# Linear attention and a SwiGLU feed-forward on one core: one block's k and v sent for ahead of a down phase, q moved by one transfer a product, basis blocks written later, the VectorE in program order

## The chip, the core and the metric

The kernel runs on one core of a Trainium2 chip. The core has five engines with a queue of instructions each: the TensorE (PE in the profile; its weight loads are PEld), the VectorE (DVE), the ScalarE (ACT), GpSimd (POOL) and SyncE (SP), which here only issues transfers. Transfers run on 16 DMA engines. SBUF is the core's working memory, PSUM holds the results of matmuls. An engine that needs another's result waits on a semaphore. The metric is the device time in microseconds of one execution.

## The reference

Eight batches, eight heads, a sequence of 576, 64 elements a head, all in FP32. Attention is linear: no softmax.

```python
kv  = np.einsum('bhsd,bhse->bhde', k, v)           # 64 x 64 per batch and head
out = np.einsum('bhsd,bhde->bhse', q, kv)
rms = np.sqrt(np.mean(out * out, axis=-1, keepdims=True) + 1e-06)
x   = (out / rms * g_norm).transpose(0, 2, 1, 3).reshape(4608, 512)
g   = x @ w_gate                                    # 512 x 1536
h   = g / (1 + exp(-g)) * (x @ w_val)               # w_val 512 x 1536
y   = h @ w_out                                     # w_out 1536 x 512
```

Nearly all the arithmetic is in the three products with the weights.

## The kernel before

**Blocks.** The 4608 tokens are nine blocks of 512. For each block the attention part makes x, then the feed-forward has an *up* phase (both products with x, SiLU and the product of the two, giving h) and a *down* phase (h times w_out). Blocks 0, 1 and 2 run alone, the rest in pairs (3, 4), (5, 6), (7, 8). The attention work for the next blocks is slipped between the feed-forward's products of the current one.

**Fewer multiplications.** Block 0's up phase is plain. Block 1's uses one level of the Strassen-Winograd scheme: seven products of sums of blocks in place of eight (L629). Block 2 and the pairs use two levels. That needs *basis blocks*, sums of sub-blocks of the weights. They are made once, during block 1, and written to a tile `w` in HBM (L970), 512 KB a transfer; two groups of them (`owed_sends`) stay in an SBUF region called `arena` at first and are written only later. Block 2 and the pairs read basis blocks back from `w` through a ring of tiles `t` (L930, L933, L941), nine deep: a read waits until the product that used the slot nine reads before is done.

**Block 2's up phase.** Twelve units; each runs seven products (L797). A result leaves PSUM by an addition on the VectorE (L132) or by a copy on the ScalarE (L811) and additions from SBUF; GpSimd does the multiplications and some additions that make h (L134, L132). The loop at L1131 does three things after each product: it makes the next pieces of sums ready (`make`), takes one *chore* from a list (a VectorE or ScalarE step of the attention for the coming block), and takes *sends* from another list. A send is one quarter transfer of q (L315), 32 of them a block, alternately on SyncE's and the ScalarE's queue. Before the change it takes two sends a product.

Units are counted from 0 here. After a unit a function from a table is called; the table's key is the number of units done, so key 6 stands between unit 5 and unit 6. `ahead` (L1278 to L1322) builds this table from the attention of block 3 (`att`) and of block 4 (`then`):

- `visits` (key 1): matmuls k^T v of block 3 (a *visit*, L352); first half of block 3's q put into the sends.
- `second` (key 2): second half of block 3's q; first half of block 4's k and v asked for (`load_kv`, L294).
- `turn` (key 5): first visit to block 4's k, v; second half of block 4's k and v asked for; block 3's two q transposes (`turn_q`, L368) put into the chores.
- keys 6 and 8: the heads' products q kv (`half`, L407) for each half of block 3, with their chores (squares L421, root L437 to L452), and the two halves of block 4's q put into the sends.
- keys 9 and 10: x transposed (`turn_x`, L467), for each half.
- `last` (key 11): second visit to block 4's k, v; the two owed groups of basis blocks written, four transfers.

A visit can only use k and v once they are in; k, v and q of a block share SBUF slots with earlier ones, so a `load_kv` also waits for the last reader of what was there.

**Down phase.** Seven products of the outer level, each of parts (L629), with a table of functions called after a product. x of the next block is multiplied with the gain (L497), placed into the layout that the two-level scheme wants by 16 transfers (`place_x`, L490), and summed. `inner_sums` makes sums of sums of block 3's x for the pair; it is called after product 5 of block 2's down phase.

**What sets the order.** The program is traced in the order in which Python runs it, and a planner then arranges each engine's instructions by its own estimate of when they can start; it may move an instruction ahead of others on its engine where no data forbids it. `tc.issue_after(i)` forbids what it encloses to stand ahead of instruction i. Transfers issued on one queue go out in that queue's order.

Of the kernel before, what the change touches and what calls it, by code (L numbers as in the profile page):

```python
# [1 line left out]

# [16 lines left out]
def kernel(  # L19
# [41 lines left out]
    nc = tc.nc  # L61
# [47 lines left out]
    def span(at, size):  # L109

        return arena[:, int(at * KIB) : int((at + size) * KIB)]
# [17 lines left out]
    PAIRED = 3  # L129
# [2 lines left out]
    add = lambda e, o, a, b: e.tensor_tensor(out=o, in0=a, in1=b, op=OP.add)  # L132
    sub = lambda e, o, a, b: e.tensor_tensor(out=o, in0=a, in1=b, op=OP.subtract)  # L133
    mul = lambda e, o, a, b: e.tensor_tensor(out=o, in0=a, in1=b, op=OP.mult)  # L134

    def ring():

        return r_pool.tile([P, 4, BLK], F32, name="r")
# [75 lines left out]
    class Att:  # L214
# [246 lines left out]
        def turn_x(self, i):  # L461
            xt = self.xts[:, i].rearrange("p t j u d -> p t j (u d)")
            for j in range(0, NS, 2):
                ps = m_psum.tile([P, 2, 2, P], F32, name="m")
                for e in range(2):
                    for t in range(2):
                        self.turned_x = nc.tensor.transpose(ps[:, e, t], xt[:, t, j + e], ident)  # L467
                self.copied = nc.scalar.activation(
                    out=self.x[:, 2 * i + j // 2], in_=ps.rearrange("p e t c -> p e (t c)"), func=ACT.Copy, scale=gain
                )  # L470
# [51 lines left out]
        def half(self, i, pools=None):  # L522
            self.product(i, pools)
            self.root(i)
            self.scale(i)
            self.halves.append(self.scaled)
# [434 lines left out]
    owed_sends = []  # L961
# [118 lines left out]
    class Ffn:  # L1080
# [27 lines left out]
        def up(self, fill):  # L1108

            self.s1 = s_pool.tile([P, NP, HB], F32, name="s1")  # L1110
            units = []
            for d in range(NP // 2):
                if self.n < DEEP:
                    units += [Up(self, 2 * d), Up(self, 2 * d + 1)]
                else:
                    shared = {}
                    units += [Inner(self, d, g, shared) for g in range(4)]
            units[0].prepare()
            last = None
            for i, this in enumerate(units):  # L1120
                if i + 1 < len(units):
                    units[i + 1].prepare()
                for unit, p in this.sequence(last):
                    if unit:
                        visited, self.visited = self.visited, None
                        with tc.issue_after(visited.ins) if visited else ExitStack():
                            unit.multiply(p)
                        self.make(4)
                        if self.chores:
                            self.chores.pop(0)()  # L1130
                        for _ in range(2):  # L1131
                            if self.sends:
                                self.sends.pop(0)()
                last = this
                fill.get(12 * (i + 1) // len(units), lambda: None)()
            self.down_ = Down(self)
            self.down_.turn_t(5)
            for unit, p in last.sequence(None):
                if unit is None:
                    last.multiply(p)  # L1140
# [109 lines left out]
    def weights(upto):  # L1250
        nonlocal rounded
        while rounded < min(upto, len(pieces)):
            load_weights(rounded + 4)
            round_w(*pieces[rounded])
            rounded += 1

    def t2(place, b22, b11):

        sub(nc.vector, place, b22, place)
        add(nc.vector, place, place, b11)  # L1260

    blocks = [Att(n) for n in range(NB)]
# [7 lines left out]
    def visit(ffn, att, gs, apart=False):  # L1270

        with tc.issue_after(ffn.multiplied.ins):
            for g in gs:
                att.kv(g, apart)
        if att.n < B:
            ffn.visited = att.positions

    def ahead(ffn, att, then):  # L1278

        def load(att, i, *pairs):  # L1280
            ffn.sends += att.quarter_steps(i, pairs, (nc.sync, nc.scalar))

        def visits():
            visit(ffn, att, (0, 1))
            load(att, 0, 0, 1)

        def second():
            load(att, 1, 0, 1)
            then.load_kv(0)

        def turn():
            visit(ffn, then, (0,), True)
            then.load_kv(1)
            ffn.chores += [lambda i=i: att.turn_q(i) for i in range(2)]

        def half(i):
            with tc.issue_after(ffn.multiplied.ins):
                att.heads(i, range(NS), (m_psum, m_psum))
            ffn.visited = att.multiplied
            ffn.chores += att.chores(i)  # L1300

        def turn_x(i):
            with tc.issue_after(ffn.multiplied.ins):
                att.turn_x(i)
            ffn.visited = att.turned_x
            if i == 1:
                ffn.chores += att.sum_steps()

        def last():
            visit(ffn, then, (1,), True)  # L1310
            while owed_sends:
                owed_sends.pop(0)()

        att.homes = {
            "qt": h_alone[:, 8:12], "sq": span(0, 8).rearrange("p (f t) -> p f t", f=4),
            "xts": span(8, 8).rearrange("p (f t) -> p f t", f=4),
        }

        return {
            1: visits, 2: second, 5: turn, 6: lambda: (half(0), load(then, 0, 0, 1)),  # L1320
            8: lambda: (half(1), load(then, 1, 0, 1)), 9: lambda: turn_x(0), 10: lambda: turn_x(1), 11: last,
        }  # L1322

    for n in range(PAIRED):
        ffn = Ffn(n, blocks[n])
        nxt = blocks[n + 1]
        if n == 0:

            with tc.issue_after(squared.ins), tc.issue_after(scaled.ins):
                weights(2)  # L1330
            ffn.plain_up(0, (0,))
            copied = blocks[0].copied
            blocks[0].turn_x(1)
            for f in range(NF):
                with tc.issue_after(blocks[0].copied.ins if f else copied.ins):
                    weights(2 * (f + 2))
                ffn.plain_up(f) if f else ffn.plain_up(0, (1,))
            weights(len(pieces))
            pairs = wo.rearrange("p (j e) d -> p e j d", e=2)
            t2(pairs[:, 0, :, HD:DM], pairs[:, 1, :, HD:DM], pairs[:, 0, :, 0:HD])  # L1340
            nxt.room = xi_alone.rearrange("p a b c -> p (a b c)")

            with tc.issue_after(sent.ins):
                for i in range(2):
                    nxt.load_kv(i)
                for i in range(2):
                    nxt.load_q(i)
            ffn.plain_end()
            for g in range(2):
                nxt.kv(g)  # L1350
            nxt.turn()
        elif n == 1:

            def third():
                visit(ffn, nxt, (0,))
                nxt.load_kv(1)

            def two_thirds():
                visit(ffn, nxt, (1,))
                for i in range(2):  # L1360
                    nxt.load_q(i)

            ffn.up({4: third, 8: two_thirds})
            nxt.turn()
            blocks[PAIRED].load_kv(0)
        else:
            ffn.up(ahead(ffn, nxt, blocks[PAIRED + 1]))
            nxt = blocks[PAIRED + 1]
            nxt.turn()
            for g in range(2):  # L1370
                blocks[PAIRED + 2].load_kv(g)
        if n:
            ffn.down_.opens = n + 1

        def inner_sums():
            with tc.issue_after(ffn.multiplied.ins):
                blocks[PAIRED].inner_sums()

        ffn.down(nxt, {5: inner_sums} if n == 2 else {})
        if n == 1:  # L1380
            blocks[PAIRED].load_kv(1)
        if n == 0:
            blocks[2].load_kv(0)

            with tc.issue_after(nxt.halves[0].ins):
                for j in range(NP // 2):
                    t2(wv[j][:, 0:2], wv[j][:, 2:4], wg[j][:, 0:2])
            with tc.issue_after(ffn.down_.s4.ins):
                for j in range(NP // 2, NP):
                    t2(wv[j][:, 0:2], wv[j][:, 2:4], wg[j][:, 0:2])  # L1390
# [60 lines left out]
```

## Time and profile before

| | us |
|---|---|
| median of 3 runs | 1029.87 |
| lowest, highest | 1029.16, 1031.26 |
| the profiled execution, own time | 1032.78 |
| its span in the profile | 1031.0 |
| TensorE busy (97% of the span) | 1000.9 |
| VectorE busy (66%) | 685.1 |
| GpSimd busy (35%) | 362.5 |
| ScalarE busy (22%) | 229.0 |
| mean granted TensorE clock, share of full speed | 0.993 |

The profile records one execution. The chain of waits follows the work that ended last back to its start and gives each engine its share. The busy times by stretch have, for each row: the stretch in us from the span's start and its length, then busy time and instructions of TensorE, its weight loads, VectorE, ScalarE and GpSimd, then the granted clock, the share of time in which the DMA engines were busy, and GB/s. A row of the timeline has the start, the duration, the engine (SPq is SyncE's queue), the line, the operation, what it writes and reads, its shape and number and, in brackets, how long the engine stood before it and what ended that. A row of waits has the instruction's engine, result and line, what it waited for, the total wait, how many there were, and the longest.

### The profile page before, as it was taken

To read this page: it belongs to the slowest core of one execution; us is meant where nothing else is said; L and a number is where in the kernel's file an instruction comes from. 1 tells how busy PE (TensorE), PEld (TensorE's weight loads), DVE (VectorE), ACT (ScalarE), POOL (GpSimd) and SP (SyncE) were. 2 spreads that over 40 slices of the span, in tenths; PEclk is the share of its full clock that TensorE was granted. 3 is DMA by queue.
4 is the path that set the end of the run, shared out by engine and by line. 5 is a ranking of instruction groups with operands and counts; after the bars stand their busy time and mean duration, and the time that the engine had idled before them with its cause. 6 is when DMAs were issued, how large, how long until landed. Compare 5 with 4: busy or idle time off the path is not lost.

```text
span 1031.0 us, 17747 instructions
## 1 busy us (share of the span) xinstructions
PE 1000.9 (97%) x6774; PEld 844.1 (82%) x6774; DVE 685.1 (66%) x1166; ACT 229.0 (22%) x357; POOL 362.5 (35%) x283
## 2 busy tenths in 40 slices
PE   5999999999978999999999999999999999999998
PEld 4544688888978988888888888888888888888887
DVE  2998788988547795666667656666776566666211
ACT  2665111221202311111211211211212112121100
POOL 0000363434024531355565102465652025556600
PEclk9999999999989999999999999999999999999999
DMA  8689543667989746586742464667403545543011
GB/s 216 203 258 262 118 91 136 223 210 207 254 178 223 220 122 162 147 231 158 179 133 62 110 135 144 163 169 181 126 10 75 120 150 162 154 143 105 1 41 41
DMA packets 255637, 155.20 MB, mean 151 GB/s; under 512 B 141632, under 2 KB 234816, under 8 KB 255552
## 3 DMA queue, kind: packets, MB, share of 16 engines
q1 hardware_dynamic: 215104, 148.95, 52.9%
q10 hardware_dynamic: 40384, 5.12, 3.2%
q8 instruction: 54, 0.88, 0.4%
q14 instruction: 31, 0.25, 0.1%
q0 software_dynamic: 64, 0.00, 0.0%
HBM read 117.97 MB, written 28.70 MB: 142 GB/s over the span
## 4 chain that ended last, share of the span: by engine, by line
PE 72%; DMA 3%; DVE 1%; SPq 0%; issue 0%; ACT 0%; ACTq 0%; DVEq 0%
PE b L797 24%; PE b L629 16%; PE c L797 12%; PE c L629 8%; PE a L797 6%; PE a L629 4%; DMA t<-w 1%; PE m L407 1%; PE m L352 1%; DMA ld<-in_v_dram 1%; DMA ld<-in_q_dram 1%; DMA w<-arena 0%; DVE r L132 0%; SPq L970 0%; PE m L467 0%
## 5 line engine op out<-in xcount | busy, mean ns | idle before, releaser
L797 PE MATMUL b<-arena,t 128*128 128x256 f32 (+1 forms) x1248 | 280.9, 364 | 11.6 <-DMA t<-w 9.2
L797 PEld LDWEIGHTS b<-arena,t 128*128 128x128 f32 x1248 | 221.9, 192 | 42.8 <-DMA t<-w 7.0
L132 POOL TENSOR_TENSOR r<-r 128x256 f32<-128x256 f32 (+1 forms) x105 | 111.8, 1066 | 300.5 <-DMA t<-w 150.8
L132 DVE TENSOR_TENSOR r<-b,r 128x512 f32<-128x512 f32 (+1 forms) x273 | 162.3, 606 | 79.6 <-PE b L797 73.9
L132 DVE TENSOR_TENSOR r<-c,r 128x512 f32<-128x512 f32 (+1 forms) x179 | 109.0, 618 | 94.3 <-PE c L797 44.4
L797 PE MATMUL c<-arena,t 128*128 128x256 f32 (+1 forms) x624 | 141.0, 363 | 0.8 <-ACT r L811 0.8
L133 POOL TENSOR_TENSOR t<-wo 128x512 f32<-128x512 f32 x54 | 79.0, 1486 | 174.7 <-DVE wo L132 107.3
L132 DVE TENSOR_TENSOR r<-a,r 128x512 f32<-128x512 f32 (+1 forms) x99 | 62.5, 631 | 105.2 <-PE a L629 66.2
L134 POOL TENSOR_TENSOR arena<-r 128x1024 f32<-128x1024 f32 (+1 forms) x46 | 96.3, 2108 | 102.2 <-DVE r L132 80.1
L797 PEld LDWEIGHTS c<-arena,t 128*128 128x128 f32 x624 | 112.3, 194 | 14.4 <-ACT r L811 1.2
L133 DVE TENSOR_TENSOR arena<-arena 128x512 f32<-128x512 f32 (+3 forms) x101 | 100.4, 1006 | 18.1 <-PE b L629 11.9
L629 PE MATMUL b<-wo,arena 128*128 128x256 f32 x432 | 99.1, 382 | 1.2 <-POOL arena L134 0.8
L629 PE MATMUL b<-t,arena 128*128 128x256 f32 x432 | 96.3, 379 | 0.0
L629 PEld LDWEIGHTS b<-wo,arena 128*128 128x128 f32 x432 | 80.9, 190 | 13.5 <-DVE arena L134 1.4
L629 PEld LDWEIGHTS b<-t,arena 128*128 128x128 f32 x432 | 81.9, 190 | 11.5 <-issue 0.2
L811 ACT COPY r<-b 128x512 f32<-128x512 f32 x63 | 36.9, 586 | 224.8 <-PE b L797 209.9
L797 PE MATMUL a<-arena,t 128*128 128x256 f32 (+1 forms) x288 | 72.2, 368 | 0.0
L797 PEld LDWEIGHTS a<-arena,t 128*128 128x128 f32 x288 | 53.1, 192 | 6.5
L629 PE MATMUL a<-wo,arena 128*128 128x256 f32 x216 | 48.4, 379 | 0.0
L629 PE MATMUL c<-t,s 128*128 128x256 f32 x216 | 48.1, 379 | 0.0
L629 PE MATMUL c<-wo,arena 128*128 128x256 f32 x216 | 48.1, 379 | 0.0
L629 PEld LDWEIGHTS a<-wo,arena 128*128 128x128 f32 x216 | 41.0, 190 | 5.6
(118 smaller groups left out, 1122.0 us busy)
## 6 DMA issues: line engine op xcount, KB each, us to landing
t<-w SPq DMA_DIRECT2D x219, 256.0 KB, 3.2
t<-w SPq DMA_DIRECT2D x75, 128.0 KB, 3.2
out_dram<-r SPq DMA_DIRECT2D x17, 512.0 KB, 2.9
ld<-in_k_dram SPq DMA_DIRECT2D x26, 288.0 KB, 5.6
ld<-in_v_dram SPq DMA_DIRECT2D x26, 288.0 KB, 6.4
ld<-in_moe_w_gate_dram SPq DMA_DIRECT2D x12, 512.0 KB, 4.8
ld<-in_moe_w_val_dram SPq DMA_DIRECT2D x12, 512.0 KB, 4.7
ld<-in_moe_w_out_dram SPq DMA_DIRECT2D x12, 512.0 KB, 5.2
```

The costliest lines, as they stand in the source:

```text
L132: add = lambda e, o, a, b: e.tensor_tensor(out=o, in0=a, in1=b, op=OP.add)
L133: sub = lambda e, o, a, b: e.tensor_tensor(out=o, in0=a, in1=b, op=OP.subtract)
L134: mul = lambda e, o, a, b: e.tensor_tensor(out=o, in0=a, in1=b, op=OP.mult)
L352: self.positions = nc.tensor.matmul(self.kv_ps[r][u * D : (u + 1) * D, g, :], lhsT=k[:, u, c, :], rhs=v[:, u, c, :], start=(c == 0), stop= ...
L407: self.multiplied = nc.tensor.matmul(self.ps[i][u][p : p + D, t, j, :], lhsT=self.qt[rows, 2 * i + t, j, p : p + D], rhs=kvs[b % 3][rows, ...
L629: self.ffn.multiplied = nc.tensor.matmul(banks[e][:, e], lhsT=lhsT, rhs=rhs, start=first and i == 0 and (e == 0 or banks[0] is not banks[1 ...
L797: self.ffn.multiplied = nc.tensor.matmul(to, lhsT=weight, rhs=self.operand(o, p), start=begins, stop=True, skip_group_check=True,)
L811: nc.scalar.copy(out=dst, in_=ps)
```

## The change

Five edits, all around blocks 1 to 3:

- *k and v of block 3.* The second half of block 3's k, v was asked for after the calls of block 1's down phase; now both halves are asked for ahead of it.
- *q.* Each product of block 2's up phase is followed by one send and not by two.
- *The table.* Both halves of block 3's q enter the sends at key 1, with the first half of block 4's k and v asked for there too. Block 4's first visit and the q transposes come at key 6 (before: 5); block 3's first half at key 7 (6), with both halves of block 4's q put into the sends there; its second half at key 9 (8); its x transposes at keys 10 and 11 (9 and 10).
- *Basis blocks.* The owed groups are written after product 1 of block 2's down phase, not after the last unit of its up phase.
- *VectorE.* A new `in_order` ties each VectorE instruction that block 2's up phase traces to the one traced before it, so that the planner keeps their order; no semaphore is involved, since they are on one engine. And `inner_sums` of block 3 must now stand behind the scaling of block 4's x (`nxt.scaled`, a VectorE instruction), where before it had to stand behind the last product of block 2's up phase (`ffn.multiplied`, a TensorE instruction).

```diff
+    @contextmanager
+    def in_order(*engines):
+
+        traced = nc.cur_bb.bb.instructions
+        last = traced[-1]
+        yield
+        start = next(k for k in reversed(range(len(traced))) if traced[k] is last) + 1
+        before = {}
+        for i in traced[start:]:
+            if engines and i.engine not in engines:
+                continue
+            if i.engine in before:
+                tc.add_manual_dep(
+                    i, before[i.engine].name,
+                    mybir.DependencyInfo(mybir.DependencyClass.NoSync, mybir.DependencyReason.DATA), reason="order",
+                )
+            before[i.engine] = i
...
-                        for _ in range(2):
-                            if self.sends:
-                                self.sends.pop(0)()
+                        if self.sends:
+                            self.sends.pop(0)()
...
         def visits():
             visit(ffn, att, (0, 1))
             load(att, 0, 0, 1)
-
-        def second():
             load(att, 1, 0, 1)
             then.load_kv(0)
...
         def last():
             visit(ffn, then, (1,), True)
-            while owed_sends:
-                owed_sends.pop(0)()
...
         return {
-            1: visits, 2: second, 5: turn, 6: lambda: (half(0), load(then, 0, 0, 1)),
-            8: lambda: (half(1), load(then, 1, 0, 1)), 9: lambda: turn_x(0), 10: lambda: turn_x(1), 11: last,
+            1: visits, 6: turn, 7: lambda: (half(0), load(then, 0, 0, 1), load(then, 1, 0, 1)),
+            9: lambda: half(1), 10: lambda: turn_x(0), 11: lambda: (turn_x(1), last()),
         }
...
-            blocks[PAIRED].load_kv(0)
+            for g in range(2):
+                blocks[PAIRED].load_kv(g)
         else:
-            ffn.up(ahead(ffn, nxt, blocks[PAIRED + 1]))
+            with in_order(nc.vector.engine):
+                ffn.up(ahead(ffn, nxt, blocks[PAIRED + 1]))
...
         def inner_sums():
-            with tc.issue_after(ffn.multiplied.ins):
+            with tc.issue_after(nxt.scaled.ins):
                 blocks[PAIRED].inner_sums()
 
-        ffn.down(nxt, {5: inner_sums} if n == 2 else {})
-        if n == 1:
-            blocks[PAIRED].load_kv(1)
+        def send():
+            while owed_sends:
+                owed_sends.pop(0)()
+
+        ffn.down(nxt, {1: send, 5: inner_sums} if n == 2 else {})
```

## The prediction, on record before the result

> **What bounds the kernel now.** I read the chain of waits first. Most of it is the TensorE:
>
> ```profile
> PE 72%; DMA 3%; DVE 1%; SPq 0%; issue 0%; ACT 0%; ACTq 0%; DVEq 0%
> ```
>
> So a change to loads and to the VectorE's order can only win where the TensorE stands still. Next the busy time by stage: block 1's down phase, block 2's up phase, block 2's down phase.
>
> ```profile
> 241.00:272.40 31.40, 31.40 (x154) 27.65 (x147) 25.68 (x48) 5.31 (x8) 6.64 (x5) 1.00 0.79 207
> 272.40:377.90 105.50, 93.49 (x1173) 88.79 (x1172) 70.93 (x122) 20.61 (x35) 37.19 (x27) 0.94 0.84 205
> 377.90:409.10 31.20, 31.20 (x145) 27.48 (x146) 21.12 (x33) 5.16 (x8) 8.26 (x6) 1.00 0.50 118
> ```
>
> The second number of each row is TensorE busy. Only the up phase has a hole: 105.50 - 93.49 = 12.0 us, and its granted clock is 0.94. Third, the TensorE's own waits and the instructions that they end at:
>
> ```profile
> PE b L797 <- DMA t<-w: 9.2, 3, 6.5
> PE b L797 <- DVE r L132: 2.4, 1, 2.4
> ```
> ```profile
> 304.70 2.99 PE L797 MATMUL b<-arena,t 128*128 128x128 f32 x12 [6.51 <-DMA t<-w]
> 333.25 0.98 PE L797 MATMUL b<-arena,t 128*128 128x128 f32 x4 [2.49 <-DMA t<-w]
> 362.94 0.71 PE L797 MATMUL b<-arena,t 128*128 128x128 f32 x4 [2.36 <-DVE r L132]
> ```
>
> Two waits are for weights, one for the VectorE. After each the clock answer reads 0.50: from 302.8 to 309.6, 333.5 to 336.9 and 364.2 to 367.6, 13.6 us, half of it lost: 6.8 us. Recoverable at most: 12.0 + 6.8 = **18.8 us**.
>
> Why are weights late? SyncE's queue before the first two waits:
>
> ```profile
> 295.50 5.01 SPq L315 DMA_DIRECT2D ld<-in_q_dram  x4
> 301.08 1.41 SPq L930 DMA_DIRECT2D t<-w  x3
> ```
> ```profile
> 325.09 3.72 SPq L315 DMA_DIRECT2D ld<-in_q_dram  x4
> 328.91 1.88 SPq L930 DMA_DIRECT2D t<-w  x3
> ```
>
> The weights stand behind q's transfers, and those wait for earlier landings: in the trace an issue waits for the landing of the transfer eight issues before it (the fourth q at 328.49 for one that landed at 328.48). From 272.4 to 358.5 there are 129 issues, 4.24 us each from issue to landing, so at most 8 / 4.24 = 1.89 a us. Units 1 to 3 hold 56, 36 and 48 matmul records of 0.112 us (eight take 0.89 in the chain), 15.7 us, and issue 32 q, 4 k/v and 11 weight transfers: 47 / 1.89 = 25 us, 9 us too long. That is the 6.5 us wait. Unit 6 (4.0 us plus some 1.3 of heads) issues 14 q and 5 weights: 10 us, the second wait.
>
> The third wait is block 3's inner sums, written in block 2's down phase but issued in unit 11 ahead of the products' additions:
>
> ```profile
> 358.62 2.14 DVE L132 TENSOR_TENSOR arena<-arena 128x896 f32<-128x896 f32 x1
> 360.68 1.61 DVE L133 TENSOR_TENSOR arena<-arena 128x896 f32<-128x896 f32 x1
> ```
>
> **What the Trainium skill says.** "TensorE: Matmul & The Clock Gate", What's actually happening: after an idle window of about 3.4 us the array runs at half clock, in windows of that length. The trace agrees on the lengths (6.8, 3.4, 3.4), though here idle stretches of 2.36 and 2.49 us were enough. "PSUM — Partial Sum Buffer", Engine vs sequencer instructions: the VectorE's queue is strict FIFO, so one waiting instruction holds all behind it; 362.94 shows it. "SBUF — State Buffer", Who interferes with whom: a VectorE instruction with two SBUF inputs is blocked while a GpSimd one reads SBUF. The trace agrees: L452, 0.17 us elsewhere, took 1.92 at 331.61 under a GpSimd operation of 2.34. "DMA: Bandwidth & Descriptors", Why small descriptors are slow: small descriptors carry a fixed overhead. q's 128-byte packets took 14.3 ns each against 57.7 for 1024 bytes, so 16384 of them over 16 engines cost 14.7 us for 2.1 MB.
>
> **The change part by part.**
>
> *k, v of block 3, second half.* One of its four issues already runs at 240.25; the other three move from 274.98 to about 241-244: 3 x 0.65 us of SyncE's queue and 3 x 1.3 us of DMA (128 packets of 2304 bytes, 162 ns each, on 16 engines). They pass the weight load at 245.65, not needed before 272, and land near 250, ahead of the 16 placements of x that begin at 251.1; the DMA share from 248 to 251 is near nothing. That cover gone, each us goes one for one into 272.4, for the inner sums end with the products there. I take 0. What it brings: both visits to block 3's k, v run in one piece, and slots come free about 4 us earlier.
>
> *q at one a product.* Block 3's 32 transfers now spread over units 1 to 5 (6.3 + 4.0 + 5.4 + 6.3 + 6.3 = 28.3 us, 1.2 more with a visit), with 4 k/v and about 20 weights: 56 / 1.89 = 30 us. It just fits, so the 6.5 us wait goes, with its 3.4 us of clock. Block 4's 32 start in unit 7, so unit 6 issues 4 k/v and 5 weights, 9 / 1.89 = 4.8 us in 5.2. But block 4's second k, v still waits there for the slots of block 3's q (both transposes), and the weights for unit 7's product 7 are behind it on SyncE: transposes done about 3 us into the unit, four issues of 0.6, then 5 us of DMA for k, v, against some 9 us to that product. Bounds 0 to 7 us; I take 2.0 idle and 1.7 of clock, **3.7 us**.
>
> *Last basis blocks.* Four transfers of 512 KB leave the up phase (355.38 to 359.10 of SyncE's queue) for the down phase, behind block 5's k, v. Their 2048-byte packets make 7.3 us of DMA. The cover: the queue is empty from 369.6 to 385.0 and x of block 4 is placed from 389.65, 11.8 us after the first product. If they run late, placing, gain and sums are late; the last sum ends at 408.97 with first use near 410, so 1 to 4 us of slack, then one for one. 0.
>
> *VectorE.* The inner sums go behind block 4's scaling, where it is idle for 9.24 us (until 398.82); their four operations take about 4.4. Saves the 2.36 us wait and 1.7 of clock. Program order adds waits. (a) Block 3's q transposes stand as unit 6's first two chores, and behind them that unit's additions, for which the TensorE waits within two products. q's last transfer goes out at unit 5's product 4, 4.8 us earlier, and takes 4.2: bounds 0 to 6, I take **1.0**. (b) A chore-filled unit: seven additions of 0.69 = 4.8, chores 2 x 0.67 + 0.35 + 9 x 0.2 + 0.69 = 4.2, so 9.0 us in unit 7 (5.4 + 1.3 of heads) and in unit 9 (6.3 + 1.3), with some 1.8 us of room in PSUM; in unit 9 GpSimd's h operations (4.7 us in two at 312.27, then 2 x 1.27) can block the refinements. Bounds 0.5 to 8, I take **3.5**. (c) Block 3's second x transposes and block 4's last visit now follow each other and share two PSUM buffers: two ScalarE copies of 0.69, **1.2**.
>
> Sum: 18.8 - 3.7 - 1.0 - 3.5 - 1.2 = **9.4 us** won. The profiled execution took 1032.78 us, its span 1031.0 and 1.8 around it; it would take 1023.4. The median shown lies 2.9 below it: 1029.87 - 9.4 = **1020.5**.
>
> **Rivals.**
>
> *All hidden (1012.5).* The new waits fall into slack and only 1 to 2 us come back. For it: from 337 to 360 the VectorE did such chores with the TensorE busy throughout. Against: there half the chores lay in unit 8, where four of seven results are ScalarE's; now they lie in unit 9.
>
> *Landings still bind (1025.5).* 30 us of issues in 28 to 29.5 is no margin; if the weights stay late as before, only the VectorE's wait goes: 2.36 + 1.7 + 0.4 = 4.5. Against: the bytes leaving the phase (three k/v, four writes) and the burst halved.
>
> *Slower (1035).* q is late and holds the VectorE. Block 3's 32 transfers took 30.2 us (278.2 to 308.4); if sharing stretches them past unit 6's first product by L, the TensorE idles about L - 1.8, plus up to 3.4 of clock, against 10.4 won without (a). With 2 us for a measurable loss it decides at L near 11, which needs 41 us for the 32. Against: nothing in the trace was that slow; a loss at several places at once would also be needed.
>
> *The change doesn't do what it says (1030).* The instruction order is set by a planner with its own due times; it may place the loads as before.
>
> **How the numbers follow.** Likeliest 0.47 (own range 1015 to 1025), all hidden 0.18, landings 0.18, slower 0.12, nothing 0.05. 1011 to 1028 leaves out the slow case, the null case and the edge of the hidden one. Within 0.2% means about 1027.8 to 1031.9, what a measurement here tells from no change. Faster 0.83, same 0.05, slower 0.12.
>
> **What would show it.** Right: the up phase of block 2 near 96 us instead of 105.5, no TensorE wait for weights over 3 us, no 128x896 operations between additions, the four basis-block writes after the phase. Step (a) shows as a VectorE wait on q's DMA at L368, (b) as TensorE waits on DVE at L132 in units 7 and 9, (c) as a wait on ScalarE before a visit. Wrong: a long L368 wait, weights still behind q, or x of block 4 late at the first pair.

## The result and the profile after

The changed kernel takes 1027.24 us (median of 13 runs, 1024.81 to 1029.27); the kernel before took 1029.89 us over the runs beside them. The ratio is 0.9974, 95% interval 0.9962 to 0.9985: faster by 2.7 us, where 9.4 was forecast. The profiled execution took 1028.97 us, its span is 1027.2 (before 1032.78 and 1031.0).

The lines of the changed file lie 18 further down: the products of block 2's up phase are L815 (before L797), those of the down phase L647 (L629), weight loads L948 and L951 (L930 and L933), q L333 (L315), x placed L508 (L490), the first copy after the placements L1075 (L1057).

The chain of waits of the changed kernel, by engine:

```profile
PE 69%; DVE 3%; DMA 3%; ACTq 1%; issue 1%; ACT 0%; SPq 0%; DVEq 0%
```

Before it had 72% TensorE and 1% VectorE: the VectorE and the ScalarE's queue now stand on the path. Next the busy time by stage, cut at the same instructions as before (block 1's down phase, block 2's up phase, its down phase):

```profile
241.00:271.30 30.30, 30.30 (x142) 26.68 (x141) 21.59 (x44) 4.36 (x7) 5.81 (x5) 1.00 0.91 226
271.30:373.70 102.40, 92.89 (x1182) 86.20 (x1180) 67.36 (x121) 20.23 (x35) 34.42 (x27) 0.98 0.74 185
373.70:405.00 31.30, 29.77 (x144) 25.87 (x139) 24.94 (x36) 5.49 (x9) 9.39 (x6) 1.00 0.70 187
```

The up phase went from 105.5 to 102.4 us; 9.5 us of TensorE hole are left of 12.0, and the clock is 0.98 in place of 0.94. The down phase took as long as before (31.3 against 31.2), but it has a hole of 1.5 us that it had not, made up by seven of its matmuls that were done in the up phase already. Of the 3.8 us by which the span fell, 0.8 lie ahead of block 2's first product (272.21 before, 271.37 after). The TensorE's waits in the stages around (block 2, both phases):

```profile
PE b L815 <- DMA t<-w: 5.3, 5, 1.8
PE b L815 <- DVE r L132: 2.0, 3, 0.9
PE b L647 <- ACT r L1075: 1.5, 1, 1.5
PE c L815 <- DMA t<-w: 0.8, 1, 0.8
PE m L485 <- ACT arena L486: 0.6, 1, 0.6
```

In place of three long waits there are a dozen short ones. Where they stand, from the timeline of the TensorE:

```profile
291.55 0.68 PE L815 MATMUL b<-arena,t 128*128 128x128 f32 x4 [1.81 <-DMA t<-w]
...
308.24 1.13 PE L815 MATMUL b<-arena,t 128*128 128x128 f32 x8 [1.42 <-DMA t<-w]
...
329.47 0.71 PE L815 MATMUL b<-arena,t 128*128 128x128 f32 x4 [1.26 <-DMA t<-w]
330.96 0.46 PE L815 MATMUL c<-arena,t 128*128 128x128 f32 x2 [0.78 <-DMA t<-w]
...
348.52 0.94 PE L815 MATMUL b<-arena,t 128*128 128x128 f32 x6 [0.93 <-DVE r L132]
350.74 0.66 PE L485 MATMUL m<-ident,arena 128*128 128x128 f32 x4 [0.61 <-ACT arena L486]
352.35 0.71 PE L815 MATMUL b<-arena,t 128*128 128x128 f32 x4 [0.52 <-DVE r L132]
```

By the number of products ahead of them, these are weights in units 3 to 5 and around the end of unit 7, then additions and a copy around unit 10. And in the down phase:

```profile
394.57 5.42 PE L647 MATMUL b<-t,arena 128*128 128x256 f32 x24 [1.53 <-ACT r L1075]
```

What that copy waits for shows in the timeline of the ScalarE, first of the changed kernel, then of the kernel before:

```profile
386.03 7.76 ACTq L508 DMA_DIRECT2D arena<-r  x8
393.84 0.59 ACT L1075 COPY r<-b 128x512 f32<-128x512 f32 x1 [13.99 <-DMA arena<-r]
```
```profile
389.95 7.29 ACTq L490 DMA_DIRECT2D arena<-r  x8
397.29 0.59 ACT L1057 COPY r<-b 128x512 f32<-128x512 f32 x1 [13.42 <-DMA arena<-r]
```

Eight placements of x, whose issues take 7.76 us of that queue (7.29 before), stand ahead of the copy. Before, the copy ended at 397.88 and the TensorE's next product came after it, without a wait, with some 0.75 us of slack:

```profile
398.62 5.34 PE L629 MATMUL b<-t,arena 128*128 128x256 f32 x24
```

After, the TensorE comes to that place 5.6 us earlier (it would start at 393.04), and the copy 3.4 us earlier.

### The profile page after: what moved, and what is told of

Its sections match the earlier page's. It is cut to its first block, busy times and chain, and to the rows that moved or that the text cites. A ratio compares the mean times of both kernels' runs of the same rounds, so it can differ in the third digit from the quotient of the medians.

```text
span 1027.2 us, 17734 instructions
## 1 busy us (share of the span) xinstructions
PE 998.6 (97%) x6774; PEld 839.1 (82%) x6774; DVE 682.8 (66%) x1166; ACT 228.8 (22%) x357; POOL 359.2 (35%) x283
## 4 chain that ended last, share of the span: by engine, by line
PE 69%; DVE 3%; DMA 3%; ACTq 1%; issue 1%; ACT 0%; SPq 0%; DVEq 0%
PE b L815 24%; PE b L647 15%; PE c L815 12%; PE c L647 7%; PE a L815 6%; PE a L647 4%; DMA t<-w 3%; PE m L425 1%; PE m L370 1%; ACTq L508 1%; DVE r L132 1%; DMA ld<-in_k_dram 0%; DVE z L439 0%; DVE arena L133 0%; DVE r L134 0%
## 5 line engine op out<-in xcount | busy, mean ns | idle before, releaser
L815 PE MATMUL b<-arena,t 128*128 128x256 f32 (+1 forms) x1248 | 280.8, 363 | 7.4 <-DMA t<-w 5.3
L815 PEld LDWEIGHTS b<-arena,t 128*128 128x128 f32 x1248 | 221.2, 191 | 39.6 <-DVE r L132 5.3
L815 PE MATMUL c<-arena,t 128*128 128x256 f32 (+1 forms) x624 | 140.8, 361 | 2.2 <-DMA t<-w 0.8
L133 POOL TENSOR_TENSOR t<-wo 128x512 f32<-128x512 f32 x54 | 76.9, 1447 | 175.8 <-DVE wo L132 105.8
L815 PEld LDWEIGHTS c<-arena,t 128*128 128x128 f32 x624 | 111.1, 191 | 16.9 <-PE b L815 1.4
L647 PE MATMUL b<-wo,arena 128*128 128x256 f32 x432 | 99.4, 382 | 0.9 <-POOL arena L134 0.8
L647 PE MATMUL b<-t,arena 128*128 128x256 f32 x432 | 96.4, 380 | 1.5 <-ACT r L1075 1.5
L647 PEld LDWEIGHTS b<-t,arena 128*128 128x128 f32 x432 | 81.8, 190 | 13.4 <-issue 2.1
L647 PEld LDWEIGHTS b<-wo,arena 128*128 128x128 f32 x432 | 80.8, 190 | 13.2 <-POOL arena L134 1.2
L815 PE MATMUL a<-arena,t 128*128 128x256 f32 (+1 forms) x288 | 72.2, 366 | 0.0
L815 PEld LDWEIGHTS a<-arena,t 128*128 128x128 f32 x288 | 52.9, 190 | 6.6
L647 PE MATMUL c<-t,s 128*128 128x256 f32 x216 | 48.5, 379 | 0.0
L647 PE MATMUL a<-wo,arena 128*128 128x256 f32 x216 | 48.4, 379 | 0.0
L647 PE MATMUL c<-wo,arena 128*128 128x256 f32 x216 | 48.1, 379 | 0.0
L647 PEld LDWEIGHTS a<-wo,arena 128*128 128x128 f32 x216 | 41.0, 190 | 5.6
```

The costliest lines, as they stand in the source:

```text
L647: self.ffn.multiplied = nc.tensor.matmul(banks[e][:, e], lhsT=lhsT, rhs=rhs, start=first and i == 0 and (e == 0 or banks[0] is not banks[1 ...
L815: self.ffn.multiplied = nc.tensor.matmul(to, lhsT=weight, rhs=self.operand(o, p), start=begins, stop=True, skip_group_check=True,)
```

## The experiments

Each ratio is to the kernel before, with its 95% interval. "Block 2" is the time in the profiled execution from the first product of its up phase to the first product of the pair: 136.8 us before, 133.6 in the changed kernel. It leaves out what differs ahead of it: apart from the two runs with q in wide packets, that first product comes between 269.6 and 272.2 us in the traces. Single executions of one kernel spread by some 2 us each way, so the medians decide and the profiles show the place.

### Which edit brings the gain

**The sums alone.** The kernel before, with one edit:

```diff
-            with tc.issue_after(ffn.multiplied.ins):
+            with tc.issue_after(nxt.scaled.ins):
                 blocks[PAIRED].inner_sums()
```

> The kernel before with one edit alone: block 3's inner sums behind the scaling of block 4's x. The prediction's step: the 2.36 us wait at 362.94, its 1.7 us of clock and 0.4 go, 4.5 us faster, near 1025.4 us. Rival: the VectorE has other work ready at that place and the wait comes back elsewhere, or the down phase gives it back: 1028 to 1030 us.

1025.56 us, ratio 0.9966 [0.9953, 0.9978]: 3.9 us, against 4.5 in the prediction; block 2 takes 130.3 us. In its waits of the TensorE in block 2 only weights are left:

```profile
PE b L797 <- DMA t<-w: 9.2, 3, 6.7
```

So this edit alone gives as much as the whole change, or more.

**All but the sums.** The changed kernel with the sums tied to the product again:

```diff
-            with tc.issue_after(nxt.scaled.ins):
+            with tc.issue_after(ffn.multiplied.ins):
                 blocks[PAIRED].inner_sums()
```

> The changed kernel with block 3's inner sums tied to the last product of the up phase again, every other edit kept. If the sums are worth their 3.9 us beside the other edits too, the others alone lose: about 1031 us. If the VectorE's program order, or the other places, keep the sums from standing before the additions anyway: 1027 us, as changed.

1032.31 us, ratio 1.0024 [1.0015, 1.0034]: the other edits by themselves make the kernel slower by 0.24%; block 2 takes 139.7 us. The program order does keep the sums from the products' additions, so the loss is elsewhere: they start at 370.76 and stand ahead of block 4's squares and scaling. x is placed later still, and the TensorE waits at the same copy:

```profile
396.54 2.04 PE L647 MATMUL b<-t,arena 128*128 128x256 f32 x4 [4.28 <-ACT r L1075]
```

and after that wait the busy times by stretch show thirteen products at half clock:

```profile
396.50:402.20 5.70, 5.66 (x13) 4.50 (x14) 1.20 (x2) 2.19 (x2) 0.00 (x0) 0.50 0.63 163
```

4.3 us and half of 5.7 are 7.1 us (1.5 in the changed kernel) in a place that the prediction put at nothing.

**The others, undone one by one** in the changed kernel. Two sends a product:

```diff
-                        if self.sends:
-                            self.sends.pop(0)()
+                        for _ in range(2):
+                            if self.sends:
+                                self.sends.pop(0)()
```

> The changed kernel with two sends of q a product again, everything else as changed. If spreading q was what shortened the weight waits of units 1 to 3, they grow again to a wait of more than 3 us and the clock falls to half after it: 1031 to 1035 us. If the calls' new places and k, v did it, and q's rate did not matter: 1026 to 1028 us.

1028.32 us, ratio 0.9992 [0.9982, 1.0001]: some 1 us slower than the changed kernel, with intervals that overlap. The long wait did not come back:

```profile
PE b L815 <- DMA t<-w: 4.7, 4, 2.3
```

Both expectations missed: q's rate matters a little at most, and spreading q is not what removed the wait of 6.5 us. In the kernel before, SyncE held q's transfers, and the weights behind them, until v had landed (its own waits in the up phase):

```profile
SPq L315 <- DMA ld<-in_v_dram: 5.6, 3, 2.7
```

3.5 of these 5.6 us lie between 296 and 306, behind block 4's k and v, which the change asks for one unit earlier. That this move split the long wait is likely; it was not tested alone.

The second half of block 3's k, v after the down phase again:

```diff
-            for g in range(2):
-                blocks[PAIRED].load_kv(g)
+            blocks[PAIRED].load_kv(0)
...
+        if n == 1:
+            blocks[PAIRED].load_kv(1)
```

> The changed kernel with the second half of block 3's k, v sent for after the down phase of block 1 again. The prediction's step puts this edit at nothing: 1026.5 to 1028 us. If three more issues at 275 and their bytes push q and the weights of units 1 to 3 back: 1028.5 to 1030 us.

1027.74 us, ratio 0.9989 [0.9979, 0.9998]. Not told from the changed kernel, as the prediction had it.

The last basis blocks in the up phase again:

```diff
             visit(ffn, then, (1,), True)
+            while owed_sends:
+                owed_sends.pop(0)()
```

> The changed kernel with the last basis blocks written at the end of the up phase again. The prediction's step puts this edit at nothing: 1026.5 to 1028 us. If the writes in the down phase are what makes the placements of x and the copy behind them late, the wait of 1.5 us at 393 goes: 1025.5 us. If in the up phase they hold up block 5's k, v and the q transposes: 1028.5 us or more.

1027.27 us, ratio 0.9979 [0.997, 0.9988], and the TensorE still waits 1.8 us for the copy at L1075. The place of these writes is worth nothing, and they are not what makes the placements late.

Without the program order:

```diff
-            with in_order(nc.vector.engine):
-                ffn.up(ahead(ffn, nxt, blocks[PAIRED + 1]))
+            ffn.up(ahead(ffn, nxt, blocks[PAIRED + 1]))
```

> The changed kernel without the program order on the VectorE. Theory A (full DMA engines cost the most): the waits for weights in units 1 to 3 and 6 stay, and the VectorE's order is worth little either way: 1026 to 1029 us. Rival C (program order costs what it was to save): the TensorE's waits for additions at unit 9 and 10, some 2.4 us with the one at 292.75, are gone: near 1024 us. If the order was what kept other VectorE work from standing before the additions, a wait of 1 to 3 us returns: 1029 to 1031 us.

1025.99 us, ratio 0.996 [0.9946, 0.9975]: 1.2 us better than the changed kernel, with intervals that overlap. The order is worth nothing that can be seen, and rather costs. Without it the wait at L1075 is gone, since block 4's transposed x is ready 3.4 us earlier (382.22 against 385.67), but the waits for the VectorE in units 9 to 11 are others, not fewer.

### What the weights wait for

Three theories: the DMA engines are full (A), eight transfers in flight set the rate whatever their size (B), the ring of nine tiles lets each weight be asked for too late (D).

**Same transfers, wider packets.** The changed kernel with q read from contiguous memory:

```diff
-                    out=to[32 * r : 32 * (r + 1), j, g0:g1],
-                    in_=q[b, 4 * i + 2 * j + h, s0 : s0 + 32 * (g1 - g0), 32 * d : 32 * (d + 1)].rearrange(
-                        "(g p) d -> p g d", p=32
-                    ),
+                    out=to[32 * r : 32 * (r + 1), j, g0:g1].rearrange("p g d -> p (g d)"),
+                    in_=q[b, 4 * i + 2 * j + h, s0 : s0 + 16 * (g1 - g0), :].rearrange(
+                        "(p x) d -> p (x d)", p=32
+                    ),
```

> The changed kernel with the same 64 transfers of q in block 2's up phase and as many bytes, but each row read from contiguous memory, in packets of 256 to 1280 bytes in place of 128. It leaves out q's right layout, so block 3 and later blocks get other numbers. Theory A (DMA engine time): q's packets cost 14.7 us of the 16 engines before and about 7 now, so the weights come sooner: the waits for weights of 6.1 us and the half clock after 330 go for the most part, 1020 to 1023 us. Rival B (eight transfers in flight, whatever their size): latency of each transfer barely moves and the weights stay late, 1026 to 1028 us.

1027.16 us, ratio 0.9971 [0.9961, 0.9981]: over the whole kernel the same as the changed one, but not place by place. The edit reaches q of every block but the first, and it leaves out q's right layout in all of them. In its profile block 2 begins 3.2 us later (274.53 in place of 271.37), after 4.9 us of new waits in block 1; it takes 129.7 us in place of 133.6, and the time from the pair to the end is 619.6 in place of 622.2. Its timeline still has the weights late:

```profile
293.39 0.68 PE L815 MATMUL b<-arena,t 128*128 128x128 f32 x4 [1.35 <-DMA t<-w]
295.90 2.79 PE L815 MATMUL c<-arena,t 128*128 128x128 f32 x12 [1.38 <-DMA t<-w]
...
328.49 0.71 PE L815 MATMUL b<-arena,t 128*128 128x128 f32 x4 [1.41 <-DMA t<-w]
```

Theory A, in the form that q's small packets are the cause, explains a part: block 2 gains 4.0 us in this execution, and its waits for weights fall from 6.1 to 4.7 us.

**Half as many transfers.** The same with two heads in one transfer, so 16 a block:

```diff
+                if j:
+                    for_ = to[32 * r : 32 * (r + 1), :, g0:g1].rearrange("p j g d -> p j (g d)")
+                    queue.dma_start(
+                        out=for_,
+                        in_=q[b, 4 * i + h : 4 * i + h + 3 : 2, s0 : s0 + 16 * (g1 - g0), :].rearrange(
+                            "j (p x) d -> p j (x d)", p=32
+                        ),
+                    )
```

> The changed kernel with q from contiguous memory in wide packets, as in the run before, and in 16 transfers a block in place of 32, each twice as large. It leaves out q's right layout, so block 3 and later blocks get other numbers. Rival B (eight transfers in flight): 31 transfers in place of 47 fit into units 1 to 3 at 1.89 a us, the weights are in time, 1020 to 1023 us. Theory D (the ring of nine tiles: a weight is asked for only once the slot of nine loads before is free, about 3 us ahead of its use, and any load beside it makes it late): 1025 to 1028 us, as with 32.

1017.43 us, ratio 0.9885 [0.9867, 0.9902]: 9.7 us less than with 32 transfers of the same bytes and the same packets. By the profiles, block 2 takes 123.2 us in place of 129.7, begins 1.7 us earlier, and from the pair to the end nothing differs (619.6 us both). Its waits for weights in block 2:

```profile
PE b L817 <- DMA t<-w: 1.8, 2, 1.6
```

and the clock is 1.00 throughout. So theory B explains the larger part. The trace shows it too: the transfers of SyncE and the ScalarE use eight completion semaphores between them, and of the changed kernel's 56 issues from 279 to 312 us 25 begin within 0.25 us of the landing of the transfer that had their semaphore before. Counted from issue to landing in the traces, over the transfers issued from 279 to 308 us:

| kernel | issued | mean us to landing | in flight | a us |
|---|---|---|---|---|
| before | 48 | 4.00 | 6.6 | 1.66 |
| changed | 48 | 4.07 | 6.7 | 1.66 |
| q wide, 32 a block | 53 | 3.58 | 6.5 | 1.83 |
| q wide, 16 a block | 43 | 4.35 | 6.5 | 1.48 |
| half of q on GpSimd | 57 | 5.34 | 10.5 | 1.97 |

"In flight" is the sum of all times to landing over the 29 us. With SyncE and the ScalarE alone it stays at 6.5 to 6.7 here (up to 7.4 in the other runs), whatever is moved. The rate is no constant: the window opens before the first of these transfers, and from the first to the last transfer of block 3's q, 281.5 to 312.2, the changed kernel issues 55, 1.79 a us. One thing is not separated: with 16 transfers half of the sends are empty, in runs of eight, so that eight products without q go ahead of every eight with it.

**Half of q on GpSimd**, in the right layout:

```diff
-            ffn.sends += att.quarter_steps(i, pairs, (nc.sync, nc.scalar))
+            ffn.sends += att.quarter_steps(i, pairs, (nc.sync, nc.gpsimd))
```

> The changed kernel with half of q's transfers in block 2's up phase issued by GpSimd in place of the ScalarE, in the right layout. Rival B (the eight transfers in flight that SyncE and the ScalarE share set the rate): GpSimd's have a count of their own, so 31 in place of 47 remain in units 1 to 3 and the weights are in time: 1019 to 1023 us. If it is the load on the DMA engines or memory after all, nothing moves: 1026 to 1028 us. If GpSimd pays over 1 us an issue and makes h late: 1029 us or more.

1025.38 us, ratio 0.9956 [0.9942, 0.9969]: 1.9 us, less than expected; block 2 takes 128.9 us. GpSimd's transfers use eight semaphores of their own. The limit on what is in flight is lifted (10.5), the waits for weights fall to 1.3 us, but each transfer takes 5.34 us. The DMA engines are now full, as the stretch from 304 to 336 shows (the last numbers: clock, DMA share, GB/s):

```profile
304.00:336.00 32.00, 30.43 (x426) 28.85 (x425) 24.23 (x46) 7.09 (x13) 24.93 (x27) 1.00 1.03 242
```

A part of what is won goes to waits for additions (4.4 us, in the changed kernel 2.4), and the copy in the down phase still costs 1.5. So theory A returns as the second limit, close behind the first.

**One tile fewer in the ring:**

```diff
-    t_pool = pool("t", 9)
+    t_pool = pool("t", 8)
...
-            while self.next and not self.held[-9]:
+            while self.next and not self.held[-8]:
```

> The changed kernel with eight tiles in the ring of weights in place of nine, in block 2 and in the pairs. Theory D (the ring sets when a weight is asked for): each weight is asked for about 1 us later, the waits for weights in block 2's up phase double to 12 us or more and the clock falls to half again: 1033 us or more. Rivals A and B (full DMA engines or eight in flight set it): 1027 to 1030 us.

1035.76 us, ratio 1.0067 [1.0044, 1.0089]. The time is as theory D said, the place is not: block 2's weights wait 6.7 us in place of 6.1, it takes 132.3 us (133.6 changed), and the first pair starts at 403.81 (405.00). From there to the end it takes 630.0 us in place of 622.2. The ninth tile is needed by the pairs; it does not set block 2's phase.

**Block 4's first k, v two units later:**

```diff
             load(att, 1, 0, 1)
-            then.load_kv(0)
...
-            1: visits, 6: turn,
+            1: visits, 3: lambda: then.load_kv(0), 6: turn,
```

> The changed kernel with the first half of block 4's k and v asked for at key 3 and not with q at key 1. If its 1.2 MB, which landed between 284 and 289, made the weights at 291 late, that wait of 1.8 us and the VectorE's of 0.5 behind it go, and at most half of it returns near unit 3: 1025 to 1026.5 us. If any load at any place delays weights that are asked for only 3 us ahead, the wait moves with it: 1027 us.

1027.25 us, ratio 0.9979 [0.9968, 0.999]. The waits near 291 are gone and one of 3.5 us stands at 303: the four transfers delay the weights wherever they stand, as a count in flight would; so would their 1.2 MB.

### The copy behind the placements

```diff
-            nc.scalar.copy(out=u3, in_=self.ps["b"])
+            (nc.vector.tensor_copy if self.ffn.n == 2 else nc.scalar.copy)(out=u3, in_=self.ps["b"])
```

> The changed kernel with one PSUM copy of block 2's down phase on the VectorE and not on the ScalarE, where it stands behind eight placements of x. If that queue is what the TensorE waits for at 393, the wait of 1.5 us goes and the pair's up phase starts 1.5 us sooner: about 1025.5 us. Rival: the sums of x, which need the placements, are late by as much, and the pair's first product waits in its place: 1027 us.

1025.56 us, ratio 0.9957 [0.994, 0.9974], 1.7 us less than the changed kernel (the intervals overlap), and no wait is left in the down phase. Without the program order as well:

> The changed kernel with neither the program order on the VectorE nor the copy on the ScalarE's queue. If both cost as much as the two runs alone said (1.2 and 1.7 us): about 1024.3 us. If the planner's order had already moved the TensorE past the copy (its profile shows no wait there): as without program order alone, 1026 us.

1025.22 us, ratio 0.9959 [0.9947, 0.9971]. The two don't add up: the planner's order had already taken that wait away.

### Combinations

The sums and GpSimd's queue on the kernel before (both edits as above):

> The kernel before with two edits: block 3's inner sums behind the scaling (1025.6 us alone), and half of q's transfers issued by GpSimd. If the transfers in flight that SyncE and the ScalarE share are what makes the weights late there (9.2 us of waits and some 5 of half clock), most of it goes: 1016 to 1019 us. If the 16 DMA engines then cap the rate at the 1.97 a us of the run with GpSimd's queue, 47 transfers take 24 us in place of 28: 1020 to 1022 us. If neither matters: 1025 to 1026 us.

1024.9 us, ratio 0.995 [0.9937, 0.9963], 0.7 us better than the sums alone. All expectations with a large gain missed. With two sends a product q's burst fills the DMA engines (0.99 from 272 to 304), and the heads of block 3 wait for the VectorE (3.3 us).

The change with GpSimd's queue and without the program order:

> The changed kernel with half of q on GpSimd (1025.4 us) and without the VectorE's program order (1.2 us faster when alone). If the waits for additions, 4.4 us in the run with GpSimd's queue, come from that order: 1022 to 1024 us. If the VectorE has no room in units 9 to 11 in either order: 1025 to 1026 us.

1025.71 us, ratio 0.9959 [0.9945, 0.9973]. Waits for weights are down to 0.4 us and waits for the VectorE up to 9 us: it is late around units 9 to 11 in either order.

The change with GpSimd's queue and the copy on the VectorE:

> The changed kernel with half of q's transfers issued by GpSimd (1025.4 us alone) and the PSUM copy of block 2's down phase on the VectorE (1.7 us faster alone). If the copy behind the placements gives back what the up phase wins, the two add up: 1023 to 1024.3 us. If the sums of x, late as well, stop the pair instead: 1025 to 1025.6 us.

1022.04 us, ratio 0.9935 [0.9917, 0.9953]: 7.7 us faster than the kernel before and 5.2 faster than the changed one, which the noise does not tell from the sum of the two, 3.6. Its TensorE is busy throughout from the last units of the up phase to the pair (the stretch from 370 to 404 us):

```profile
370.00:404.00 34.00, 34.00 (x159) 29.78 (x158) 28.34 (x41) 5.58 (x8) 8.33 (x6) 1.00 0.66 185
```

It is faster than both kernels.

## Why the prediction came out as it did

The direction was right, and 1027.24 lies inside the range of 1011 to 1028, but outside the likeliest case's own 1015 to 1025. By its steps, in lost time of the profiled execution:

| step | predicted us | measured us |
|---|---|---|
| lost time that could come back | 18.8 | |
| left in units 1 to 5 (weights) | 0 | 5.4 |
| left after unit 6 (idle 2.0, clock 1.7) | 3.7 | 4.1 |
| (a) q transposes | 1.0 | 0.3 |
| (b) VectorE, from unit 7 on | 3.5 | 2.4 |
| (c) two ScalarE copies | 1.2 | 0.8 |
| down phase | 0 | 1.7 |
| gain | 9.4 | 4.1 |

The measured column adds, at each wait shown above, what the start of the next matmul lies further off than the matmul's own time: in units 1 to 5, 1.97 at 291 and 0.68 behind it (an addition, late by the same stop), 0.66 at 299, 0.53 at 301, 1.58 at 308. 18.8 less 14.7 is 4.1; block 2 became 3.1 us shorter, the span 3.8, the median 2.7. The up phase took 102.4 us where 96 was named.

**The step that failed: "It just fits, so the 6.5 us wait goes".** The mechanism, an issue that waits for the landing of the one eight before, is what the runs show: on top of wide packets, halving the count brought block 2 from 129.7 to 123.2 us. The sum was mis-sized. Its own 30 us stood against 28.3, or 29.5 with the visit, so it did not fit, and it is an average over units 1 to 5. One send a product still puts 21 of q into units 1 to 3, with 4 k/v and the 11 weights counted there: 36 transfers, 19.0 us at 1.89 a us, an estimate from the prediction's figures, against 15.7 us of products. The four k/v go first and take 3.8 to 6.3 us to land (280.44 to 284.26, 282.47 to 288.81), and the weights behind them are late for the product at 291. In sum 5.4 us were lost where nothing was put. The rate itself was nearly right, 1.79 a us. And the wait of 6.5 us, though gone, did not go because q was spread: it stayed away with two sends as well.

That the clock stayed up after these waits was in part luck. At the same place a wait of 1.9 us in the run with the copy on the VectorE, and one of 1.7 with the writes in the up phase, were followed by 3.4 us at half clock; 1.81 here and 1.8 without the program order were not.

**The down phase at nothing.** The prediction asked when the placements' *sums* were due and found 1 to 4 us. It did not ask what stands behind the placements on the queue that issues them. The copy at L1057 had 0.75 us. The cause is not the basis blocks (writing them in the up phase leaves the wait), but that the TensorE gained 5.6 us and the chain of block 4's squares, scaling and transposes on the VectorE, which the placements need, only 3.9 (they begin at 386.03 on that queue in place of 389.95), and their issues took 0.5 longer. The program order has a part in that: without it the transposes end 3.4 us earlier and the wait is gone. The 4.3 us at this copy without the moved sums, and the times with the copy on the VectorE, show that a part of the gain of the up phase is given back here.

**Right:** the sums, 3.9 of 4.5. (The sums that ran ahead of the additions at 362.94 were at work from 358.62 to 362.29, not waiting; the queue's order did the rest.) k and v of block 3, and the writes, at nothing, though the writes' 1024 packets of 2048 bytes took 87 ns each in the trace, 5.6 us of 16 engines and not 7.3.

**Right in size, not in reason:** the 3.7 us after unit 6, with 1.26 and 0.78 us idle and one stretch of 3.4 us at half clock. The weights there were to stand behind block 4's second k, v, and these behind block 3's q transposes, which end at 319.02. SyncE's queue shows the k, v going out before that:

```profile
315.36 1.26 SPq L312 DMA_DIRECT2D ld<-in_k_dram  x2
316.67 1.91 SPq L312 DMA_DIRECT2D ld<-in_v_dram  x2
320.94 5.61 SPq L948 DMA_DIRECT2D t<-w  x3
```

The last of these three weights goes out at 326.18, right after a transfer of block 4's q had landed at 326.12, and lands itself at 329.43, for the product at 329.47: eight in flight again, and not the slots. Luck, then, for the number.

**Right in place in part:** of the VectorE's terms (a) to (c), 2.2 us too large together, (a) and (c) came where they were put; (b) came in one place, around unit 10, and not in unit 7.

**The rivals.** "Landings still bind" (1025.5) came nearest, with the sums as the only gain; its weights did become less late, and what they gave went to the VectorE's order and the copy. "All hidden", "slower" and "does not do what it says" did not occur; without the sums the other edits end on the slower side (1032.31), for a reason that was not among the rivals.

What stays open: how much of the step from 32 to 16 transfers is the count and how much the products without q; what the table's new places are worth, which were never undone as a whole; and why single executions of one kernel spread by 2 us each way. Two parts of that spread show in the traces: block 2 begins anywhere within 2.6 us, and a wait of the same length is followed by half clock in one execution and not in another.

## What to carry to other kernels

When transfers in flight set the rate, count transfers as well as bytes, and count them unit by unit: a sum that just fits over five units is a miss in the first three. Before an engine that is ahead is made faster still, look for the next thing that it waits for in the following stage, on each queue that this thing stands in: here 0.75 us of slack behind eight issues on the ScalarE gave back a good part of the gain. Try each edit of a bundle alone: here a single one brought all of the gain, and the rest together lost.

## What the runs showed that was not expected

- Equal bytes in equal packets: 16 transfers in place of 32 a block are worth 9.7 us, 6.5 of them in block 2. Wider packets at equal count change nothing in the median (1027.16 against 1027.24), but the profile has 4.0 us less in block 2 and 2.6 less from the pair on against 3.2 more ahead of block 2.
- Transfers issued by GpSimd take 0.60 us of it each and do not count against what SyncE and the ScalarE have in flight: 10.5 in flight in place of 6.7, 1.97 a us in place of 1.66, at 5.34 us each in place of 4.07.
- The granted clock fell to half for 3.4 us at 332, after idle stretches of 1.26 and 0.78 us with some work between. A single wait of 1.7 to 1.9 us at 291 was followed by such a stretch in two runs and by none in the changed kernel.
